# A fused attention and gated-MLP kernel: inverse root of the norm by one power operation on POOL, and other places for some steps of the third block

## Chip, core and metric

The kernel runs on one core of one Trainium2 chip. The metric is the device time of one execution in microseconds (us). TensorE is called PE here, its weight loads PEld; VectorE is DVE, ScalarE is ACT, GpSimd is POOL and SyncE is SP.

## The reference, cut to what matters

```python
def _attn_ref(q, k, v, g_norm):                  # q, k, v: (8, 8, 576, 64)
    kv = np.einsum('bhsd,bhse->bhde', k, v)
    out = np.einsum('bhsd,bhde->bhse', q, kv)
    rms = np.sqrt(np.mean(out * out, axis=-1, keepdims=True) + 1e-06)
    return out / rms * g_norm

def _moe_ref(x, w_gate, w_val, w_out, w_res):    # x: (4608, 512), d_ff 1536
    g = x @ w_gate
    gelu = 0.5 * g * (1.0 + erf(g / sqrt(2)))
    ffn_out = gelu * (x @ w_val) @ w_out
    res_gate = 1.0 / (1.0 + np.exp(-(x @ w_res)))
    return x + res_gate * ffn_out
```

Linear attention for 8 batches of 8 heads, an RMS norm over the 64 elements of each head and token, and a gated MLP with a gated residual over all 4608 tokens. The step that the change is about is the inverse root: for each token and head, (sum of squares / 64 + 1e-6) to the power of -0.5.

## The kernel before, in words

The tokens are cut into nine blocks: blocks 0 to 7 hold the first 512 tokens of each batch (NJ = 4 tiles of 128), block 8 holds the 64 tokens that each batch has left over. Every block goes through the gate and value products with a GELU, and through the output product. Matrix products from block 2 on are done with sums of quadrants (seven products in the place of eight), so DVE has to make sums of activations and weights: `ts` (token_sums, L896), `ws` (weight_sums, L870), `hid_s` (s_sum, L496).

Attention for batch b is computed two blocks ahead, in the middle of block m = b - 2 (`plan_attn_ahead`, L1389; batches 1 and 2 have plans of their own, L1314 and L1359). The order of the work is written out by hand: `at` puts a step behind a slot of a block, `aside_out` ahead of a product of the output stage (`others`, L709, with the places "F", "00", "22", "01", "11", "end"), and `at_word` behind a word of the list `ORDERS` (L911) of a group of gate and value products. There are three such groups per block. Each engine then works through its own list in that order. A step that is put earlier on DVE holds up all that stands behind it on DVE.

The words that matter: "Fg" and "Fv" are the additions of DVE in L967 that give a PSUM bank F from A and a kept tile d; "cg" and "cv" the same with the tile c; "h11", "h12", "h21" are multiplications on DVE, "h22" one on POOL (L983), which write the hidden layer; "7g" and "7v" are products of PE that write the bank that "Fg" and "Fv" have read.

The attention steps, with their lines:

- `a_sq` (L253, ACT) squares o, `a_red` (L258, DVE) sums each head into `ss`.
- `a_norm` (L295) makes `rinv` (shown as the tile `ny`) of `ss`. On POOL these are twelve instructions: L306 gives m = ss/64 + eps (tile `nm`), L307 a first guess from the bits of m, L312 to L319 two steps (tiles `na`, `nh`). On DVE there are also twelve, with three steps (L321 to L325). Batch 1 has its norm on DVE, batches 2 to 7 on POOL; for batches 3 to 7 it is put ahead of place "F" of the output stage of block b - 2.
- `a_t` (L345, DVE) multiplies a PSUM tile of o by `rinv` and writes `t`. There are four per batch, t(0) to t(3), and a fifth for the left-over rows from batch 4 on. `a_t` is the last reader of its PSUM bank: the banks of o(0) and o(1) are the banks Fg and Fv of the next block's first group.
- `d_xT` (L387) is a transposing DMA on SP's queue from `t` to `xT`; `a_g` (L370, DVE) scales `xT` in place by the norm's weight g; the products and the `ts` sums read the scaled `xT`.
- In the output stage (`others`) DVE makes wF (L714), c22 (L724, tile `osb` from `wA` and `wd`), the gatings of L698 and the `ts` sums of the next block in between; POOL makes the gating of (1,1) (L732, the tile `osb` from `th` and `osb`), which reads c22, and then `row_times_g` (L361).

The third block is block 2, the first that is done in groups throughout (`WHOLE` = 2): its attention is that of batch 2, its `ts` sums are made in the output stage of block 1, and t(2), t(3), the transposing DMA and `a_g` of batch 3 lie in its groups.

Of the kernel before, what the change touches and what calls it, by code (L numbers as in the profile page):

```python
# [7 lines left out]

FP32 = mybir.dt.float32
FP16 = mybir.dt.float16  # L10
I32 = mybir.dt.int32
AF = mybir.ActivationFunctionType
ALU = mybir.AluOpType

# [4 lines left out]
def kernel(  # L19
# [15 lines left out]
    nc = tc.nc  # L35
    P = nc.NUM_PARTITIONS
    B, H, S, D = q.shape
    C = H * D
    F = moe_w_gate.shape[1]
    NP = H // 2  # L40
    NF = F // P
    NJ = 4
# [6 lines left out]
    consts = ctx.enter_context(tc.tile_pool(name="consts", bufs=1))  # L49
# [242 lines left out]
                out=o32.rearrange("p (r e d) -> p r e d", e=2, d=D)[:, :, e, :], in_=st[b]["ps"][1][e]  # L292
            )

    def a_norm(b, j0, j1, eng=nc.vector):  # L295

        s = st[b]
        if "rinv" not in s:
            s["rinv"] = attnp.tile([P, NJ + 1, H], FP32, tag="ny", name="ny")
        ss, yy = (t[:, j0:j1, :].rearrange("p j h -> p (j h)") for t in (s["ss"], s["rinv"]))  # L300
        n = (j1 - j0) * H
        m = attnp.tile([P, (NJ + 1) * H], FP32, tag="nm", name="nm")[:, 0:n]
        a = attnp.tile([P, (NJ + 1) * H], FP32, tag="na", name="na")[:, 0:n]
        mh = attnp.tile([P, (NJ + 1) * H], FP32, tag="nh", name="nh")[:, 0:n]
        magic = 0x5F1FFFF9 if eng is nc.gpsimd else 0x5F3759DF
        eng.tensor_scalar(out=m, in0=ss, scalar1=1.0 / D, scalar2=RMS_EPS, op0=ALU.mult, op1=ALU.add)  # L306
        eng.tensor_scalar(  # L307
            out=yy.bitcast(I32), in0=m.bitcast(I32), scalar1=-0.5, scalar2=float(magic), op0=ALU.mult, op1=ALU.add
        )
        if eng is nc.gpsimd:  # L310
            for step in range(2):
                eng.tensor_tensor(out=a, in0=yy, in1=yy, op=ALU.mult)  # L312
                eng.tensor_tensor(out=a, in0=a, in1=m, op=ALU.mult)
                c = (-0.703952253, 0.703952253 * 2.38924456) if step == 0 else (0.375, -1.25)
                eng.tensor_scalar(out=mh, in0=a, scalar1=c[0], scalar2=c[1], op0=ALU.mult, op1=ALU.add)
                if step == 1:
                    eng.tensor_tensor(out=mh, in0=mh, in1=a, op=ALU.mult)
                    eng.tensor_scalar(out=mh, in0=mh, scalar1=1.875, scalar2=None, op0=ALU.add)
                eng.tensor_tensor(out=yy, in0=mh, in1=yy, op=ALU.mult)  # L319
            return  # L320
        eng.tensor_scalar(out=mh, in0=m, scalar1=-0.5, scalar2=None, op0=ALU.mult)  # L321
        for _ in range(3):
            eng.tensor_tensor(out=a, in0=yy, in1=yy, op=ALU.mult)
            eng.tensor_tensor(out=a, in0=a, in1=mh, op=ALU.mult)
            eng.scalar_tensor_tensor(out=yy, in0=a, scalar=1.5, in1=yy, op0=ALU.add, op1=ALU.mult)  # L325

    def pair(b):

# [5 lines left out]
    def a_t(b, i):  # L334

        o, rinv = st[b]["o"][i], st[b]["rinv"]
        if i < NJ:
            jj, e = i // 2, i % 2
            t = t_t[b][:, 2 * jj : 2 * jj + 2, :].rearrange("p j (r e d) -> p j r e d", e=2, d=D)[:, :, :, e, :]
            scale = of_o(rinv, i)[:, :, :, None].to_broadcast([P, 2, NP, D])  # L340
        else:
            t = t_t[B][:, pair(b), :].rearrange("p (h d) -> p h d", h=H)
            o = o.rearrange("p (h d) -> p h d", h=H)
            scale = rinv[:, NJ, :, None].to_broadcast([P, H, D])
        nc.vector.tensor_tensor(out=t, in0=o, in1=scale, op=ALU.mult)  # L345
# [17 lines left out]
    def a_g(b, j0, j1, eng=nc.vector):  # L363

        blk, k0 = where(b, j0)
        xs = xT_t[blk][:, k0 : k0 + j1 - j0, :, :]
        if eng is nc.scalar:
            nc.scalar.activation(out=xs, in_=xs, func=AF.Copy, scale=gcol)
        else:
            eng.tensor_scalar(out=xs, in0=xs, scalar1=gcol, scalar2=None, op0=ALU.mult)  # L370
# [659 lines left out]
    for which in "kv":  # L1030
        if which == "k":
            t = hidp.tile([P, NF, NJ * P], FP16, tag="hid", name=which + "f").rearrange("p a b -> p (a b)")
        else:
            t = hid_s
# [51 lines left out]
    nc.vector.memset(mask[D : 2 * D, D : 2 * D], 1.0)  # L1086
    eps_col = consts.tile([P, 1], FP32, name="eps_col")
    nc.vector.memset(eps_col, RMS_EPS)
    ones16 = consts.tile([1, P], FP16, name="ones16")
    nc.vector.memset(ones16, 1.0)  # L1090
    one32 = consts.tile([1, 1], FP32, name="one32")
# [264 lines left out]
    def aside_out(blk, ahead_of, *fs):  # L1356
        amid_out.setdefault(blk, {}).setdefault(ahead_of, []).extend(fs)

    def plan_attn_2():  # L1359
        b, m = 2, 1  # L1360
        act = nc.scalar.copy
        at(m - 1, 2 * NF + 3, lambda: by_token(b, act, slice(0, 2)))
        at(m, 0, lambda: by_token(b, act, slice(2, 4)), lambda: attn_begin(b), lambda: d_qT(b))
        at(m, 2, lambda: a_kv(b))
        at(m, 3, lambda: load_behind(b))
        at(m, 1, lambda: wo_sums(1))
        at(m, 3, lambda: wo_sums(3))
        at(m, 4, lambda: a_o(b))
        for j in range(NJ):
            at(m, 4 + j // 2, lambda j=j: a_ss(b, j))  # L1370
        at(m, 6, lambda: a_norm(b, 0, NJ, nc.gpsimd))
        for j in range(NJ):
            at(m, 9 + j // 2, lambda j=j: a_t(b, j))
        at(m, 10, lambda: d_xT(b, 0, NJ))
        for i in range(2):
            aside_out(m, "F", lambda i=i: a_g(b, 2 * i, 2 * i + 2))

    WHOLE = 2
    GROUPS = {blk: (1, 2) for blk in range(2, WHOLE)} | {blk: (0, 1, 2) for blk in range(WHOLE, B - 1)} | {B - 1: (1, 0, 2), B: (0, 1, 2)}
# [2 lines left out]
    def at_word(blk, i, word, *fs):  # L1382
        amid_gv.setdefault((blk, i), {}).setdefault(word, []).extend(fs)
# [5 lines left out]
    def plan_attn_ahead(b):  # L1389

        rem = pair(b) is not None
        m = b - 2
        assert rem == (m in GROUPS)
        act, pool = nc.scalar.copy, nc.gpsimd
        begin = [lambda: attn_begin(b), lambda: d_qT(b)]
        if rem:
            at_word(m, 0, "h22", begin.pop(0), lambda: d_rem_qT(b))
        if m in GROUPS:
            for i in range(2):
                half = lambda i=i: by_token(b, act, slice(2 * i, 2 * i + 2))  # L1400
                if whole(m):
                    at_word(m, i, "g11", half)
                else:
                    at(m, 2 + i, half)
            if whole(m):
                at_word(m, 1, "g11", *begin)
            else:
                at(m, 3, *begin)
            if b + 1 < B:
                at(m, 2 * GF, lambda: load_behind(b))  # L1410
            last = len(GROUPS[m]) - 1
        else:
            at(m, 8, lambda: by_token(b, act, slice(0, 2)))
            at(m, 9, lambda: by_token(b, act, slice(2, 4)), *begin)
            at(m, NF - 1, lambda: a_kv(b, act))
            at(m, NF, lambda: load_behind(b))
        if rem:
            at_word(m + 2, 0, "cv", lambda: a_g(b, NJ, NJ + 1))
            own = 2 * pair(b) + 1 == b
            at_word(m, last, "5v" if own else "3g", lambda: a_rem_kv(b))  # L1420
            at_word(m, last, "dv" if own else "g12", lambda: kv_out(b))
            if own:
                at_word(m, last, "3g", lambda: rem_mm(b))
            at_word(m, last, "g12", lambda: rem_out(b))
        else:
            at(m, NF, lambda: a_o(b), lambda: a_ss(b, 0), lambda: a_ss(b, 1))
            aside_out(m, "D", lambda: a_ss(b, 2), lambda: a_ss(b, 3))
        aside_out(m, "F", lambda: a_norm(b, 0, NJ + rem, pool))
        first = [lambda: new_block(b), lambda: a_t(b, 0), lambda: a_t(b, 1)]
        if whole(m + 1):  # L1430
            aside_out(m, "01" if m + 1 == WHOLE else "11", *first[0:2])
            amid_out[m].setdefault("end", []).insert(0, first[2])
        else:
            at(m, NF + 3, *first)
        if whole(m + 1):
            t = [lambda j=j: a_t(b, j) for j in range(NJ)]
            if rem:
                at_word(m + 1, 0, "h21", lambda: a_t(b, NJ), lambda: d_xT(b, NJ, NJ + 1))
            for i, word, fs in (
                (0, "1v", t[2:3]),  # L1440
                (0, "Fv", [t[3], lambda: d_xT(b, 0, NJ)]),
                (1, "cv", [lambda: a_g(b, 0, 2)]),
                (2, "Fv", [lambda: a_g(b, 2, NJ)]),
            ):
                at_word(m + 1, i, word, *fs)
            return
        for j in range(2, NJ + rem):
            at(m + 1, j - 2, lambda j=j: a_t(b, j))
        at(m + 1, 1, lambda: d_xT(b, 0, NJ))
        at_word(m + 1, 1, "Fv", lambda: a_g(b, 0, 2))  # L1450
        at_word(m + 1, 1, "cv", lambda: a_g(b, 2, NJ))
# [184 lines left out]
```

## Time and profile before

| what | us |
|---|---|
| median of 3 runs | 321.48 (321.4 to 321.97) |
| the profiled execution | 321.97, of it span 320.2 |
| PE busy | 311.9 (97% of the span) |
| DVE busy | 274.6 (86%) |
| ACT busy | 210.8 (66%) |
| POOL busy | 187.2 (58%) |
| mean granted PE clock | 0.995 |

The page gives for each engine the busy time, then the span in 40 slices, then the chain of waits that ended last, then groups of equal instructions with their mean duration and the idle time ahead of them. A timeline gives instructions in order of time: start, duration, engine, line, operation, out<-in, and in brackets the idle time before and who ended it. Ends of matmuls are modelled, so a wait of PE shows best in the distance between the starts of two groups of matmuls: four matmuls of 256 columns start 0.44 us apart from the next four when nothing holds them up, twelve start 1.31 us apart.

### The profile page before, as it was taken

Reading aid. Unit: us, or ns where it says so; the run is one execution under the profiler, and the core shown is the slowest. Engines: PE = TensorE matmul, PEld = TensorE weight load, DVE = VectorE, ACT = ScalarE, POOL = GpSimd, SP = SyncE. Lnnn points to the kernel's source line nnn. Section 1 sums busy time; section 2 is a strip of 40 time slices with the busy share of each in tenths; the row PEclk is TensorE's granted clock in tenths of the full one; section 3 lists DMA queues with packets and bytes.
Section 4 is the critical chain, followed back from the end, with each engine's and each line's share of the span. In section 5 each row is a group of like instructions: output and inputs, shape, how many; then the busy total and the mean of one; then the engine's idle time right before and its main releaser. Section 6 shows DMA issues by size and latency. Waiting matters only on the chain.

```text
span 320.2 us, 7756 instructions
## 1 busy us (share of the span) xinstructions
PE 311.9 (97%) x3044; PEld 247.5 (77%) x3044; DVE 274.6 (86%) x486; ACT 210.8 (66%) x385; POOL 187.2 (58%) x249
## 2 busy tenths in 40 slices
PE   8989999999999999999999999999999999999993
PEld 3544755444788888888888888888888888888882
DVE  5788889799888899989998999799988777897774
ACT  3673684465847795878587858795768467836760
POOL 2792350572869378757875777517761375396332
PEclk9999999999999999999999999999999999999998
DMA  8999999799994899479947894800340003001204
GB/s 251 328 204 204 195 204 190 168 155 178 176 106 82 199 130 105 82 215 120 112 82 217 109 124 69 227 6 0 69 147 2 0 3 134 0 2 44 89 2 131
DMA packets 76694, 38.90 MB, mean 122 GB/s; under 512 B 42098, under 2 KB 74354, under 8 KB 76658
## 3 DMA queue, kind: packets, MB, share of 16 engines
q0 software_dynamic: 38752, 17.17, 42.4%
q1 hardware_dynamic: 37328, 20.71, 25.3%
q8 instruction: 24, 0.39, 0.5%
q10 hardware_dynamic: 578, 0.52, 0.5%
q14 instruction: 12, 0.10, 0.1%
HBM read 38.80 MB, written 9.44 MB: 151 GB/s over the span
## 4 chain that ended last, share of the span: by engine, by line
PE 96%; DVE 2%; issue 0%; ACT 0%; DVEq 0%
PE Av L946 12%; PE Ag L946 12%; PE wA L515 12%; PE Fv L946 6%; PE Fg L946 6%; PE gps L410 5%; PE vps L410 5%; PE rA L566 4%; PE fps L447 3%; PE Ev L946 3%; PE Eg L946 3%; PE wD L515 3%; PE wF L515 3%; PE wE L515 3%; PE w L515 2%; PE idle L1111 2%
## 5 line engine op out<-in xcount | busy, mean ns | idle before, releaser
L983 POOL TENSOR_TENSOR hid<-ge,c 128x512 f16<-128x512 f16 x22 | 25.6, 1162 | 40.2 <-ACT ge L977 40.2
L515 PEld LDWEIGHTS <-hid_s 128*128 128x128 f16 x384 | 37.6, 98 | 4.5 <-issue 0.2
L946 PEld LDWEIGHTS <-wsv 128*128 128x128 f16 x352 | 34.0, 98 | 5.6 <-issue 1.3
L946 PEld LDWEIGHTS <-wsg 128*128 128x128 f16 x352 | 34.4, 98 | 4.1
L361 POOL TENSOR_TENSOR t<-t,g 128x512 f16<-128x512 f16 x32 | 37.1, 1189 | 0.0
L702 POOL TENSOR_TENSOR osb<-osb,t 128x512 f32<-128x512 f32 x28 | 34.0, 1244 | 0.0
L956 ACT COPY Eg<-Ag 128x512 f32<-128x512 f32 x22 | 12.9, 585 | 27.8 <-PE Ag L946 27.8
L515 PEld LDWEIGHTS <-hid 128*128 128x128 f16 x288 | 28.2, 98 | 3.5
L946 PEld LDWEIGHTS <-wg 128*128 128x128 f16 x264 | 25.8, 98 | 3.2
L946 PEld LDWEIGHTS <-wv 128*128 128x128 f16 x264 | 25.8, 98 | 3.0
L946 PE MATMUL Av<-ts,wsv 128*128 128x256 f16 x176 | 26.4, 272 | 0.2 <-ACT Ev L956 0.2
L946 PE MATMUL Ag<-ts,wsg 128*128 128x256 f16 x176 | 26.4, 273 | 0.0
L967 DVE TENSOR_TENSOR Fg<-Ag,d 128x512 f32<-128x512 f32 x22 | 15.3, 696 | 12.3 <-ACT d L960 7.6
L258 DVE TENSOR_REDUCE ss<-sq 128x8 f32<-128x512 f32 x32 | 20.5, 679 | 1.7 <-ACT sq L253 1.7
L398 ACT ACTIVATE ge<-gps 128x512 f16<-128x512 f32 x20 | 11.8, 599 | 14.2 <-PE gps L410 14.0
L515 PE MATMUL wA<-wo_ts,hid_s 128*128 128x256 f16 x168 | 20.6, 273 | 0.0
L977 ACT ACTIVATE ge<-Eg 128x512 f16<-128x512 f32 x22 | 13.2, 598 | 10.0 <-PE Eg L946 10.0
L977 ACT ACTIVATE ge<-c 128x512 f16<-128x512 f32 x22 | 13.8, 627 | 7.8 <-DVE c L967 7.8
L345 DVE TENSOR_TENSOR t<-op,ny 128x512 f16<-128x512 f32 x28 | 18.4, 684 | 0.5 <-POOL ny L319 0.4
L977 ACT ACTIVATE ge<-Fg 128x512 f16<-128x512 f32 x22 | 13.0, 591 | 8.6 <-PE Fg L946 6.6
L967 DVE TENSOR_TENSOR c<-Ag,d 128x512 f32<-128x512 f32 x22 | 15.2, 689 | 4.1 <-PE Ag L946 4.1
L410 PE MATMUL gps<-xT,wg 128*128 128x512 f16 x72 | 18.5, 379 | 0.0
(219 smaller groups left out, 860.2 us busy)
## 6 DMA issues: line engine op xcount, KB each, us to landing
out_dram<-osb SPq DMA_DIRECT2D x14, 512.0 KB, 3.6
qraw<-in_q_dram POOLq DMA_DIRECT2D x7, 512.0 KB, 6.8
k<-in_k_dram POOLq DMA_DIRECT2D x7, 512.0 KB, 8.7
v<-in_v_dram POOLq DMA_DIRECT2D x7, 512.0 KB, 10.5
wg<-in_moe_w_gate_dram POOLq DMA_DIRECT2D x2, 512.0 KB, 8.4
wv<-in_moe_w_val_dram POOLq DMA_DIRECT2D x2, 512.0 KB, 8.8
wo<-in_moe_w_out_dram POOLq DMA_DIRECT2D x2, 512.0 KB, 13.9
out_dram<-osb SPq DMA_DIRECT2D x4, 256.0 KB, 4.5
```

What stands on the lines that cost most here:

```text
L258: nc.vector.tensor_reduce(out=out_, in_=sqs.pop((b, i)), op=ALU.add, axis=mybir.AxisListType.X)
L345: nc.vector.tensor_tensor(out=t, in0=o, in1=scale, op=ALU.mult)
L361: eng.tensor_tensor(out=t_t[blk][:, jj, :], in0=t_t[blk][:, jj, :], in1=g16, op=ALU.mult)
L410: nc.tensor.matmul(ps[:, j0 * P : j1 * P], lhsT=w[:, cc, :], rhs=xT_t[blk][:, j0:j1, cc, :], start=(cc == 0 and j0 == 0), stop=(cc == NP - ...
L515: nc.tensor.matmul(ps[:, e - es[0], :], lhsT=a[:, f, e * P : (e + 1) * P], rhs=b[:, f, :], start=(start and e == es[0] and f == 0), stop=( ...
L566: nc.tensor.matmul(out_[:, e, :], lhsT=x_[:, e, cc, :], rhs=w_[:, cc, :], start=(first and e == 0 and cc == 0), stop=(cc == 1), skip_group ...
L702: nc.gpsimd.tensor_tensor(out=res_all[of], in0=res_all[of], in1=t_t[blk][of], op=ALU.add)
L946: nc.tensor.matmul(out_[:, r, :], lhsT=lhsT, rhs=rhs, start=(first and r == 0 and c == 0), stop=(c == 1), skip_group_check=True,)
L956: nc.scalar.copy(out=tile_of("E", u), in_=ps["A", u])
L967: nc.vector.tensor_tensor(out=dst, in0=ps["A", u], in1=sb["d", u], op=ALU.add)
L977: nc.scalar.activation(out=ge[q], in_=source(q, "g"), func=AF.Gelu)
L983: eng.tensor_tensor(out=dst, in0=ge[q], in1=source(q, "v"), op=ALU.mult)
```

## The change

- `a_norm` has two instructions in the place of twelve, both on POOL: m = ss/64 + eps, and then one tensor_tensor with the power operation, m to the power of a constant tile `minus_half`. That tile, 128x40 of -0.5, is written once by a memset on DVE in the opening.
- The norm of batch 1 moves from DVE to POOL (the default engine of `a_norm`).
- In the output stage of block 1, the two scalings `a_g` of batch 2 stood ahead of DVE's wF; they now stand behind it, ahead of the `ts` sums.
- In block 2, for batch 3: t(2) goes from behind "1v" to behind "Fv" of group 0, t(3) and the transposing DMA from behind "Fv" to behind "cv", and the first `a_g` from behind "cv" of group 1 to behind "h21" of group 1.

The instructions of PE, ACT and SP stand in the same order as before. DVE has 11 instructions fewer, POOL 58 fewer.

```diff
-    def a_norm(b, j0, j1, eng=nc.vector):
+    def a_norm(b, j0, j1, eng=nc.gpsimd):
...
         m = attnp.tile([P, (NJ + 1) * H], FP32, tag="nm", name="nm")[:, 0:n]
-        a = attnp.tile([P, (NJ + 1) * H], FP32, tag="na", name="na")[:, 0:n]
-        mh = attnp.tile([P, (NJ + 1) * H], FP32, tag="nh", name="nh")[:, 0:n]
-        magic = 0x5F1FFFF9 if eng is nc.gpsimd else 0x5F3759DF
         eng.tensor_scalar(out=m, in0=ss, scalar1=1.0 / D, scalar2=RMS_EPS, op0=ALU.mult, op1=ALU.add)
-        eng.tensor_scalar(
-            out=yy.bitcast(I32), in0=m.bitcast(I32), scalar1=-0.5, scalar2=float(magic), op0=ALU.mult, op1=ALU.add
-        )
...
-                eng.tensor_tensor(out=yy, in0=mh, in1=yy, op=ALU.mult)
-            return
...
+        eng.tensor_tensor(out=yy, in0=m, in1=minus_half[:, 0:n], op=ALU.pow)
...
+    minus_half = consts.tile([P, (NJ + 1) * H], FP32, name="minus_half")
+    nc.vector.memset(minus_half, -0.5)
...
-            aside_out(m, "F", lambda i=i: a_g(b, 2 * i, 2 * i + 2))
+            amid_out.setdefault(m, {}).setdefault("00", []).insert(i, lambda i=i: a_g(b, 2 * i, 2 * i + 2))
...
+            first_whole = m + 1 == WHOLE
             for i, word, fs in (
-                (0, "1v", t[2:3]),
-                (0, "Fv", [t[3], lambda: d_xT(b, 0, NJ)]),
-                (1, "cv", [lambda: a_g(b, 0, 2)]),
+                (0, "Fv" if first_whole else "1v", t[2:3]),
+                (0, "cv" if first_whole else "Fv", [t[3], lambda: d_xT(b, 0, NJ)]),
+                (1, "h21" if first_whole else "cv", [lambda: a_g(b, 0, 2)]),
                 (2, "Fv", [lambda: a_g(b, 2, NJ)]),
```

More of the change, by code (lines that the diff above doesn't have):

```diff
@@ L10 @@
 FP16 = mybir.dt.float16
-I32 = mybir.dt.int32
 AF = mybir.ActivationFunctionType
@@ L302, in a_norm @@
         m = attnp.tile([P, (NJ + 1) * H], FP32, tag="nm", name="nm")[:, 0:n]
-        a = attnp.tile([P, (NJ + 1) * H], FP32, tag="na", name="na")[:, 0:n]
-        mh = attnp.tile([P, (NJ + 1) * H], FP32, tag="nh", name="nh")[:, 0:n]
-        magic = 0x5F1FFFF9 if eng is nc.gpsimd else 0x5F3759DF
         eng.tensor_scalar(out=m, in0=ss, scalar1=1.0 / D, scalar2=RMS_EPS, op0=ALU.mult, op1=ALU.add)
-        eng.tensor_scalar(
-            out=yy.bitcast(I32), in0=m.bitcast(I32), scalar1=-0.5, scalar2=float(magic), op0=ALU.mult, op1=ALU.add
-        )
[L310 to L319, printed above, removed]
-            return
[L321 to L325, printed above, removed]
+        eng.tensor_tensor(out=yy, in0=m, in1=minus_half[:, 0:n], op=ALU.pow)
     def pair(b):
```

## The prediction, made before the changed kernel had run

> **What bounds the kernel now.** First the page: busy times and the 40 slices.
>
> ```profile
> PE 311.9 (97%) x3044; PEld 247.5 (77%) x3044; DVE 274.6 (86%) x486; ACT 210.8 (66%) x385; POOL 187.2 (58%) x249
> ...
> PE   8989999999999999999999999999999999999993
> ```
>
> PE is the bound from slice 3 on. A shorter norm gains nothing by itself: only a place where PE stands still can give time back. The list of waits names 0.2 us of idle PE behind the opening, but modelled ends hide more, so I read PE's timeline for starts that lie over 0.44 us (four matmuls) or 1.31 us (twelve) apart. The third block and the stage ahead of it have some:
>
> ```profile
> 86.19 1.47 PE L515 MATMUL wE<-wo,hid 128*128 128x256 f16 x12
> 87.67 1.47 PE L515 MATMUL wA<-wo_ts,hid_s 128*128 128x256 f16 x12
> ...
> 94.69 0.60 PE L946 MATMUL Ev<-xT,wv 128*128 128x256 f16 x4
> 95.25 0.60 PE L946 MATMUL Ag<-ts,wsg 128*128 128x256 f16 x4
> 95.85 0.60 PE L946 MATMUL Av<-ts,wsv 128*128 128x256 f16 x4
> ...
> 105.99 0.60 PE L946 MATMUL Ag<-ts,wsg 128*128 128x256 f16 x4
> 106.79 0.60 PE L946 MATMUL Av<-ts,wsv 128*128 128x256 f16 x4 [0.20 <-ACT Ev L956]
> ```
>
> 1.48 in place of 1.31, 0.56 and 0.60 in place of 0.44, 0.80 in place of 0.44: 0.17 + 0.12 + 0.16 + 0.36. Smaller ones at 97.63 (0.03), 105.54 (0.05) and 108.63 (0.09) make it 0.98 us. Then the output stage of a later block (2; blocks 3 to 5 look alike 32.5 us apart), DVE, POOL and PE in this order:
>
> ```profile
> 120.46 0.97 DVE L478 TENSOR_TENSOR hid_s<-hid,hid_s 128x1536 f16<-128x1536 f16 x1
> ...
> 122.64 0.68 DVE L478 TENSOR_TENSOR osb<-wA,wd 128x512 f32<-128x512 f32 x1
> ...
> 123.83 0.41 DVE L478 TENSOR_TENSOR ts<-xT,ts 128x512 f16<-128x512 f16 x1
> 124.17 0.68 DVE L698 TENSOR_TENSOR osb<-th,wF 128x512 f32<-128x512 f32 x1
> ...
> 126.00 1.28 DVE L345 TENSOR_TENSOR t<-op,ny 128x512 f16<-128x512 f32 x2
> ```
>
> ```profile
> 119.76 0.22 POOL L306 TENSOR_SCALAR nm<-ss 128x40 f32<-128x40 f32 x1 [2.15 <-DVE ss L258]
> 120.06 0.22 POOL L307 TENSOR_SCALAR ny<-nm 128x40 int32<-128x40 int32 x1
> ...
> 124.50 0.27 POOL L319 TENSOR_TENSOR ny<-nh,ny 128x40 f32<-128x40 f32 x1
> 124.73 1.27 POOL L698 TENSOR_TENSOR osb<-th,osb 128x512 f32<-128x512 f32 x1
> ```
>
> ```profile
> 126.13 0.60 PE L946 MATMUL Ag<-ts,wsg 128*128 128x256 f16 x4
> 126.74 0.60 PE L946 MATMUL Fv<-ts,wsv 128*128 128x256 f16 x4
> ```
>
> DVE works without a break from 120.46 to t(1), 126.00 to 126.69, and Fv starts 0.05 us behind it, 0.17 late (0.61 in place of 0.44): Fv's bank is that of o(1), which t(1) reads last. So in these four stages DVE's list up to t(1) is on the path that sets the end, with no slack. POOL's gating `osb<-th,osb` stands behind the norm; its input, c22, has been there since 123.32.
>
> [...]
>
> ```profile
> 281.11 0.78 DVE L478 TENSOR_TENSOR ts<-xT,ts 128x512 f16<-128x512 f16 x1
> ...
> 103.40 1.49 DVE L370 TENSOR_SCALAR xT<-xT,gcol 128x1024 f16<-128x1024 f16 x1
> ```
>
> The first takes 0.42 us by itself; a POOL multiplication ended at 281.60, and it ended 0.28 later. The second takes 0.48 elsewhere. With short POOL operations the hold is smaller (`hid_s` above met one until 120.62 and took 0.97 in place of 0.95).[...]
>
> **The change, part by part.**
>
> *The power.* Below: as cheap as a plain operation of that shape, 0.27 us (`ny<-nh,ny`, median of 12). Above: as dear as the eleven instructions that it replaces, 120.06 to 124.77, 4.7 us; nothing excludes more. A plain operation costs (1244 - 270)/(512 - 40) = 2.1 ns per element, so 40 elements are 0.08 of the 0.27 and 0.19 is fixed. I take five times the work per element: 0.19 + 0.41 = 0.6 us. The five is a choice.
>
> *Stages of blocks 2 to 5 (batches 4 to 7), in the times of block 2.* The power runs 120.06 to 120.66[...]; `hid_s`[...] starts at 120.66 in place of 120.46. Behind it, with the undisturbed steps of this list (0.90, three ts of 0.34): c22 at 122.58 to 123.26 (before 122.64: the short POOL operations had cost DVE some 0.25). Then comes the collision. `ny` is ready at 120.7, so `osb<-th,osb` no longer waits for it but starts when c22 is there (+0.09, as `nm` behind `ss`): 123.35 to 124.62. DVE's next `ts`[...] wants to start at 123.77, is held until 124.62 and ends 0.28 later, 124.90. The next starts at 124.82 (before 124.17); t(0) 125.43, gating 126.04, t(1) 126.64 to 127.33, Fv 127.38 in place of 126.74: +0.64. Four stages: **+2.6 us**. With 0.27 for the power c22 is bound by PE (122.47), Fv comes at 127.27: 4 x 0.53 = +2.1. Each further us of the power adds about 1 per stage.
>
> *Stage of block 1, third block.* wF ahead of the scalings ends by 87.2 in place of 87.61, which PE waited for (0.17). The scalings then wait for the power (86.61 to 87.21) and end near 88.1, two ts near 88.8, c22 starts at 88.9 when PE lets it, 0.4 ahead of need. POOL's gating runs near 89.7 to 91[...]. t(2) behind "Fv": "Fg" starts 0.6 earlier, which 7g and 7v waited for (0.12, 0.16, 0.03). t(3) 1.2 later, and its DMA with it: landings take at most 6.3, and `a_g` comes 8 us later; on SP's queue nothing due stands behind it. `a_g` out of "cv": the hidden products no longer stand behind 1.49 us, Ev's seed is in time (0.05, 0.36, 0.09). At "h21" it meets POOL's `hid` (105.14 to 106.3 before) and ends just as "Fg" may start; I take **-0.9** of the 0.98.
>
> *Batch 1.* The chain on DVE runs 47.54 to 49.97, t at 50.07. On POOL: `nm` at 47.61, power 47.91 to 48.51, t near 48.6. PE's transposes stand behind a run of output matmuls and start at 51.46 without a gap: nothing gained. Nothing lost up to a power of 2.1 us; from there each us is lost on PE. POOL is idle there from 44.8 to 55.3, only the store's additions stand behind. DVE waits in t, ahead of the sums of w_out, which now come earlier.
>
> *Batch 2.* t starts at 74.70, 0.7 behind `ny`: no gain, no loss.
>
> *The memset*: at most 0.11 us (a 64x64 one); hidden by the warm-up matmuls ahead of PE's first transposes at 5.84; without that cover 0.1.
>
> Sum: +2.6 - 0.9 = +1.7. The profiled execution (span 320.2, time 321.97, 0.49 above the median) would become 323.7; on the median 321.48 + 1.7 = **323.2**. A measurement here can tell about 0.2%, 0.64 us.
>
> **The rivals.**
>
> *A. Faster: the gating doesn't hold `ts`* (it starts too late[...]). For it: DVE is up to 0.3 us ahead by then, and short POOL operations hold it little. Against: four `ts` near 280 were each held by POOL multiplications. Then t(1) ends some 0.1 earlier than before: -0.9 - 4 x 0.1 = -1.3, **320.2**. It decides at Fv: below +0.22 us per stage (0.9/4) the kernel gets faster.
>
> *B. No change*: held in part, +0.2 per stage: -0.1, 321.4.
>
> *C. The power is slow.* For it: no operation of this kind is in the trace[...]; against: nothing. At 2.0 us `hid_s` starts at 122.06, t(1) ends at 128.73, Fv +2.04, four times 8.2; c22 of block 1 is late by 0.75: +8.05, **329.5**. At 4.7 us it is some 4.7 per stage, 3 in block 1 and 2.6 for batch 1: near 345.
>
> **How the numbers follow.** Forecast (power 0.27 to 1.2 us, collision) 0.48, from 322.7 to 325.6; A 0.14; B 0.11; C 0.27. Range 320.8 to 330: it leaves out half of A and half of C. Faster 0.14, same 0.11, slower 0.75.
>
> **What would show it.** POOL's `osb<-th,osb` near 123.4 and the `ts` behind it 1.1 us long; Fv of the first group over 1 us behind Ag; `hid_s` at the power's end; PE's late starts of the third block gone. A power over 1.2 us, or a `ts` of 0.42 us there, would make the forecast wrong.

## The result, and the profile after

The changed kernel takes 334.35 us (median of 4 runs, 333.31 to 338.45) against 321.46. It is 1.0387 times as long, 95% interval 1.034 to 1.0433; this ratio leaves out the slow run of 338.45, whose granted clock was 0.983 in place of 0.996. The forecast was 323.2 with 320.8 to 330 as its range, slower with 0.75. The direction was right and the time was missed by 11 us. The profiled execution took 333.31 us, 11.34 us more than that of before, with a span of 331.5.

PE's work is the same (311.7 us busy, before 311.9), and its share has dropped:

```profile
PE 311.7 (94%) x3044; PEld 246.8 (74%) x3044; DVE 272.4 (82%) x475; ACT 210.4 (63%) x385; POOL 208.5 (63%) x191
...
PE   8899996999989997999799998999799999999993
```

In the row of slices 6, 7 and 8 stand where 9 stood, six times: PE stands still at six places inside the span. POOL is busier by 21 us, although it has 58 instructions fewer. The view of the tile `ny` says why; its columns are least, median and largest duration in ns:

```profile
L303 POOL TENSOR_TENSOR ny<-nm,minus_half x7: 5457/6764/6788, 47.2 to 227.2; 128x40 f32<-128x40 f32 x4, 128x32 f32<-128x32 f32 x3
```

One power takes 5.46 us for 32 columns and 6.78 us for 40: longer than the eleven instructions that it replaced (4.7 us). What that does is seen in the output stage of block 2, the one shown for before (3.05 us later here: `nm` at 122.81 against 119.76). First POOL, then DVE, then PE:

```profile
122.81 0.22 POOL L302 TENSOR_SCALAR nm<-ss 128x40 f32<-128x40 f32 x1 [2.11 <-DVE ss L257]
123.11 6.79 POOL L303 TENSOR_TENSOR ny<-nm,minus_half 128x40 f32<-128x40 f32 x1
129.88 1.26 POOL L676 TENSOR_TENSOR osb<-th,osb 128x512 f32<-128x512 f32 x1
```

```profile
123.51 0.95 DVE L456 TENSOR_TENSOR hid_s<-hid,hid_s 128x1536 f16<-128x1536 f16 x1
...
126.70 0.42 DVE L456 TENSOR_TENSOR ts<-xT,ts 128x512 f16<-128x512 f16 x1
127.04 0.68 DVE L676 TENSOR_TENSOR osb<-th,wF 128x512 f32<-128x512 f32 x1
129.93 0.69 DVE L323 TENSOR_TENSOR t<-op,ny 128x512 f16<-128x512 f32 x1 [2.22 <-POOL ny L303]
```

```profile
128.31 0.60 PE L924 MATMUL Av<-xT,wv 128*128 128x256 f16 x4
130.68 0.60 PE L924 MATMUL Fg<-ts,wsg 128*128 128x256 f16 x4 [1.77 <-DVE t L323]
131.11 0.60 PE L924 MATMUL Ag<-ts,wsg 128*128 128x256 f16 x4
131.88 0.60 PE L924 MATMUL Fv<-ts,wsv 128*128 128x256 f16 x4 [0.16 <-DVE t L323]
```

t(0) waits 2.22 us for the power. Before, it started without a wait:

```profile
124.80 0.69 DVE L345 TENSOR_TENSOR t<-op,ny 128x512 f16<-128x512 f32 x1
```

The bank of t(0) is the bank of Fg, so Fg starts 2.37 us behind Av in place of 0.44, and Fv waits another 0.33 for t(1). DVE's list ahead of that wait runs undisturbed: `hid_s` starts 0.40 us into the power and takes 0.95, `ts` takes 0.42. Where batch 1's norm now stands on POOL, PE's transposes wait as well (timeline of PE, 46 to 56 us; first before, then after):

```profile
51.46 0.61 PE L352 MATMUL xtp<-ident,t 128*128 128x128 f16 x8
```

```profile
54.08 0.62 PE L330 MATMUL xtp<-ident,t 128*128 128x128 f16 x8 [3.12 <-DVE t L323]
```

The sum over the span, from the distances between the starts of PE's matmuls in the two profiles:

| where | before | after | difference, us |
|---|---|---|---|
| batch 1, transposes | 0 | 3.29 | +3.29 |
| first group of block 2: Fg, Ag, Fv | 0.04 | 1.47 | +1.43 |
| first groups of blocks 3 to 6: Fg, Fv | 0.70 | 9.03 | +8.33 |
| late starts ahead of and in the third block | 0.98 | 0 | -0.98 |
| opening, up to 20 us | 7.33 | 6.63 | -0.71 |

Together +11.36 of the 11.34. The opening's share is not of the change: it varies between runs of one kernel (7.33 us in the profile of before, 7.44 in that of e11, 6.64 in that of e7, which share its opening). The large terms are all waits of t for the power.

### The profile page after: what moved, and what is told of

The parts are those of the page before. It is cut to its first block, busy times and chain, and to the rows that moved or that the text cites. A ratio compares the mean times of both kernels' runs of the same rounds, so it can differ in the third digit from the quotient of the medians.

```text
span 331.5 us, 7687 instructions
## 1 busy us (share of the span) xinstructions
PE 311.7 (94%) x3044; PEld 246.8 (74%) x3044; DVE 272.4 (82%) x475; ACT 210.4 (63%) x385; POOL 208.5 (63%) x191
## 4 chain that ended last, share of the span: by engine, by line
PE 73%; DVE 9%; POOL 8%; ACT 3%; issue 2%; DMA 2%; SPq 1%; DVEq 0%; POOLq 0%; ACTq 0%
PE Ag L924 11%; PE Av L924 11%; POOL ny L303 8%; PE Fv L924 6%; PE Fg L924 6%; PE wA L493 5%; PE gps L388 5%; PE vps L388 5%; PE rA L544 3%; PE Ev L924 3%; PE Eg L924 3%; PE w L493 2%; PE rps L408 2%; PE rF L544 2%; PE kvp L207 2%
## 5 line engine op out<-in xcount | busy, mean ns | idle before, releaser
L303 POOL TENSOR_TENSOR ny<-nm,minus_half 128x40 f32<-128x40 f32 (+1 forms) x7 | 43.5, 6216 | 0.6
L924 PE MATMUL Fg<-ts,wsg 128*128 128x256 f16 x88 | 13.2, 272 | 7.4 <-DVE t L323 7.4
```

The lines of the kernel that those rows point to most:

```text
L303: eng.tensor_tensor(out=yy, in0=m, in1=minus_half[:, 0:n], op=ALU.pow)
L924: nc.tensor.matmul(out_[:, r, :], lhsT=lhsT, rhs=rhs, start=(first and r == 0 and c == 0), stop=(c == 1), skip_group_check=True,)
```

## The experiments

Theory 1: the loss is the time at which `ny` is ready for t, and nothing else; the other places of the third block's steps gain about 0.9 us. The first rival was the forecast's own mechanism, the collision of POOL's early gating with DVE's `ts`; the second, that the power's long run holds DVE or POOL's later work. All ratios are to the kernel before on the same chip.

**e1_places: the places without the power.** The kernel before with the two parts of the diff that move steps:

```diff
-            aside_out(m, "F", lambda i=i: a_g(b, 2 * i, 2 * i + 2))
+            amid_out.setdefault(m, {}).setdefault("00", []).insert(i, lambda i=i: a_g(b, 2 * i, 2 * i + 2))
...
-                (0, "1v", t[2:3]),
+                (0, "Fv" if first_whole else "1v", t[2:3]),
...
```

> The third block's other places alone; the norm stays as before (guess and steps, batch 1 on DVE). Theory 1 (all of the loss is the wait for the power): the late starts of PE ahead of and in the third block (0.98 us in the profile of before) go, about 0.9 us faster than before, 320.5. Rival (the places themselves cost something, or gain nothing): 321.5 or more.

Measured 0.997 (0.9956 to 0.9984), 320.99 against 321.8: as theory 1 expected. The same kernel ran once more for a profile.

**e11_places_again: the same kernel.**

> The third block's places alone once more, for a profile of it beside that of before: the late starts of PE at wA behind wE, at 7g and 7v of group 0 and at Av behind Ev's seed (0.98 us in the profile of before) are gone, and 0.997 of before as in the first series; if the gain comes from elsewhere, these starts are still late.

Measured 0.9965 (0.9948 to 0.9983). The same places in PE's timeline as in the prediction (0.9 to 1.0 us later here at the first of them), where the starts were 1.48, 0.56, 0.60 and 0.80 us apart:

```profile
87.15 1.47 PE L515 MATMUL wE<-wo,hid 128*128 128x256 f16 x12
88.46 1.47 PE L515 MATMUL wA<-wo_ts,hid_s 128*128 128x256 f16 x12
...
95.47 0.60 PE L946 MATMUL Ev<-xT,wv 128*128 128x256 f16 x4
95.91 0.60 PE L946 MATMUL Ag<-ts,wsg 128*128 128x256 f16 x4
96.35 0.60 PE L946 MATMUL Av<-ts,wsv 128*128 128x256 f16 x4
...
106.39 0.60 PE L946 MATMUL Ag<-ts,wsg 128*128 128x256 f16 x4
106.83 0.60 PE L946 MATMUL Av<-ts,wsv 128*128 128x256 f16 x4
```

1.31, 0.44, 0.44 and 0.44: all four are gone. This version, guess and steps with the new places, is faster than both kernels; it takes 0.35% less time than the one before.

**e2_power: the power without the places.** The changed kernel with those two parts of the diff taken back.

> The power operation alone, all places as before. Theory 1: the loss of the changed kernel and the gain of the places that is then missing, +12.5 to +13 us on before, about 334.2. Rival (part of the loss comes from the places): less than +12, below 333.5.

Measured 1.0504 (1.0481 to 1.0526), 338.11 us: more than either theory expected. The row of PE's clock in its page, and PE's timeline at the two places where a digit of it drops:

```profile
PEclk9999997999999999999999997999999999999998
```

```profile
54.80 1.03 PE L330 MATMUL xtp<-ident,t 128*128 128x128 f16 x8 [3.13 <-DVE t L323]
55.63 1.91 PE L425 MATMUL fps<-wo,hid 128*128 128x512 f16 x4
```

```profile
204.20 1.01 PE L924 MATMUL Fv<-ts,wsv 128*128 128x256 f16 x4 [0.16 <-DVE t L323]
205.00 1.06 PE L924 MATMUL Av<-ts,wsv 128*128 128x256 f16 x4
205.86 1.06 PE L924 MATMUL Eg<-xT,wg 128*128 128x256 f16 x4
```

Four matmuls of 256 columns take 0.86 us in place of 0.44 here. PE's granted clock was 0.51 from 54.00 to 57.50 us (PE still waited, until 54.80) and 0.50 from 204.20 to 207.60, and 1.00 from 57.50 to 61.00 and from 201.00 to 204.20. By the distances between the starts of matmuls the two stretches cost 1.28 and 1.67 us. The profiled execution of the changed kernel has no such stretch (1.00 from 20 to 320 us), and this one's span is 4.9 us longer. The rest of the 4.9 is the missing gain of the places (1.0 us in its profile: 0.16 + 0.13 + 0.16 + 0.37 and three starts below 0.1), 0.1 at Fg of the first group of block 2, and 0.75 in the opening. So the places' gain holds with the power too; the clock was in neither theory.

**e3_product: a short operation in the power's place.** The inverse root is left out.

```diff
-        eng.tensor_tensor(out=yy, in0=m, in1=minus_half[:, 0:n], op=ALU.pow)
+        eng.tensor_tensor(out=yy, in0=m, in1=minus_half[:, 0:n], op=ALU.mult)
```

> The changed kernel with a product in the place of the power: same instructions, queues and waits, but ny is -m/2, so the inverse root is left out and the output is not the reference's. It is the short operation of 0.27 us that my forecast reckoned with. Theory 1 (only the time at which ny is ready counts): no loss is left and the places' gain stays, 320.6 or less. Rival (the collision of the forecast: the gating on POOL starts earlier and holds the ts sum of DVE in four stages, 0.53 us each): 322.7, with ts rows of about 1.1 us near the gating.

Measured 1.003 (1.0017 to 1.0043), 322.91 us against 321.8. A product of the same tiles takes 0.27 us (median of seven) where the power took 6.78, and most of the loss is gone. But the rival came true: with a `ny` that is ready early the kernel is still slower than before, although it keeps the places' gain. DVE and POOL in the output stage of block 2, then PE:

```profile
121.44 0.68 DVE L676 TENSOR_TENSOR osb<-th,wE 128x512 f32<-128x512 f32 x1
122.03 1.17 DVE L456 TENSOR_TENSOR ts<-xT,ts 128x512 f16<-128x512 f16 x1
123.13 0.67 DVE L676 TENSOR_TENSOR osb<-th,wF 128x512 f32<-128x512 f32 x1
```

```profile
121.66 1.27 POOL L676 TENSOR_TENSOR osb<-th,osb 128x512 f32<-128x512 f32 x1 [2.94 <-issue]
```

```profile
123.64 0.60 PE L924 MATMUL Av<-xT,wv 128*128 128x256 f16 x4
124.46 0.60 PE L924 MATMUL Fg<-ts,wsg 128*128 128x256 f16 x4 [0.22 <-DVE t L323]
124.89 0.60 PE L924 MATMUL Ag<-ts,wsg 128*128 128x256 f16 x4
125.65 0.60 PE L924 MATMUL Fv<-ts,wsv 128*128 128x256 f16 x4 [0.16 <-DVE t L323]
```

POOL's gating no longer stands behind a long norm and starts at 121.66. DVE's `ts`, 0.42 us by itself, takes 1.17: it ends 0.27 behind the gating's end (122.93). Fg comes 0.38 late and Fv 0.33, together 0.71 in place of 0.17: +0.53 per stage. The forecast's step for the cheapest power had +0.53.

**e8_product_sum_end: the same with the collision taken away.** The fourth `ts` sum goes from place "01" to "end", behind t(1); the inverse root is left out as in e3.

```diff
-        for key, f in zip(("00", "00", "22", "01") if whole(blk) else ("00", "22", "01", "11"), t):
+        for key, f in zip(("00", "00", "22", "end") if whole(blk) else ("00", "22", "01", "11"), t):
```

> The product in the place of the power (the inverse root left out, as before), and the fourth ts sum moved behind t(1), out of the way of the early gating. Collision theory: the 0.38 + 0.33 us at Fg and Fv of four stages (2.8 us) go, 322.5 - 2.8 = 319.7; up to 320.7 if the sum is now held by the multiplications by g behind the gating and makes Fg late. Rival (these late starts are not of the held sum): 322.5.

Measured 0.9971 (0.9959 to 0.9984): the late starts at Fg and Fv are gone in all four stages, a smaller one (0.16 at a later Av) has come. In the stage of block 2:

```profile
124.17 0.60 PE L924 MATMUL Av<-xT,wv 128*128 128x256 f16 x4
124.61 0.60 PE L924 MATMUL Fg<-ts,wsg 128*128 128x256 f16 x4
125.04 0.60 PE L924 MATMUL Ag<-ts,wsg 128*128 128x256 f16 x4
125.48 0.60 PE L924 MATMUL Fv<-ts,wsv 128*128 128x256 f16 x4
```

The loss of e3 was the collision's.

**e4_split: the power in two instructions.**

```diff
-        eng.tensor_tensor(out=yy, in0=m, in1=minus_half[:, 0:n], op=ALU.pow)
+        for c in (slice(0, 2 * H), slice(2 * H, n)):
+            eng.tensor_tensor(out=yy[:, c], in0=m[:, c], in1=minus_half[:, c], op=ALU.pow)
```

> The changed kernel with the power in two instructions, first the 16 columns that t(0) and t(1) read, then the rest: as much work on POOL and one instruction more. By the two shapes measured, 5.46 us for 32 and 6.78 for 40 columns, 16 take about 2.8 us. Theory 1 (the time at which t(0) and t(1) get their ny): in the four stages ny is there 2.8 us behind nm, ahead of need, so their 2.27 us each go; batch 1 keeps 2 to 3 us; in all 322 to 323.5. Rival (the time that POOL is busy or holds DVE counts): no faster than the changed kernel, about 333.

Measured 1.0158 (1.0135 to 1.0182), 327.26 us. POOL is as busy as in the changed kernel (210.8 us), and 7 us have gone: not POOL's load but the time of `ny` counts. It is 4 us above my expectation, which had left out the second half of the columns. DVE in the stage of block 2, where the second power ends at 128.67:

```profile
127.31 0.68 DVE L324 TENSOR_TENSOR t<-op,ny 128x512 f16<-128x512 f32 x1
128.70 0.69 DVE L324 TENSOR_TENSOR t<-op,ny 128x512 f16<-128x512 f32 x1 [0.71 <-POOL ny L304]
```

t(2) now waits, with the additions Fg and Fv behind it on DVE, and PE's next products start 0.21 and 0.17 late. Three more starts are late in block 3 (0.09 to 0.31) and in each of blocks 4 to 6 (0.13 to 0.26); their cause is not followed here. Batch 1 keeps 0.77 + 1.56 us at its two transposes.

**e6_first_on_dve: batch 1's norm back on DVE.**

```diff
-            NF + 6: [lambda: a_norm(b, 0, NJ), t[0], t[1], t[2], t[3]],
+            NF + 6: [lambda: a_norm(b, 0, NJ, nc.vector), t[0], t[1], t[2], t[3]],
```

with the guess and the three steps for DVE in `a_norm` again.

> The changed kernel with the norm of batch 1 on DVE by guess and steps again, as before; the power for batches 2 to 7. Theory 1 (each norm's loss is its own wait): the 3.3 us that PE stands still ahead of batch 1's transposes go, 333.3 - 3.3 = 330.0. Rival (batch 1's loss is caught up later, or the power's load counts elsewhere): 332 or more.

Measured 1.0325 (1.0287 to 1.0362), 332.3 us, 330.44 to 334.21. In its profile the late start of the transposes is gone, all 3.29 us of it, and the terms of the other batches are the same to about 0.01 us; but it has one stretch of half clock (1.67 us; the granted clock of its span is 0.991 in place of 0.996) and a start 0.7 late near 43 us that the profile of the changed kernel lacks, so its span is only 0.9 shorter. The lowest runs of the two kernels differ by 2.9 us, about the 3.3 expected; the medians by 2.05. By times alone the size is only roughly confirmed, and the rival's 332 isn't excluded by them; the profile decides for theory 1.

**e7_sum_end and e9_sum_fv: can the faster version gain more?** e11 with the fourth `ts` sum at "end" (as in e8), or behind "Fv" of the next block's first group.

The edit of e9:

```diff
-        for key, f in zip(("00", "00", "22", "01") if whole(blk) else ("00", "22", "01", "11"), t):
+        for key, f in zip(("00", "00", "22", "Fv") if whole(blk) else ("00", "22", "01", "11"), t):
+            if key == "Fv":
+                at_word(blk, 0, key, f)
+                continue
```

> Guess and steps, the new places, and the fourth ts sum moved behind t(1). DVE's list up to t(1) is 0.34 us shorter in four stages, and Fv starts 0.17 late there: 4 x 0.17 = 0.7 faster than the places alone (0.997 of before), 0.995. Rival (the sum meets POOL's multiplications by g at its new place, is held up to 1.2 us and makes Fg late): 0.997 or more.

> As the one before, but the fourth ts sum stands behind Fv of the next block's first group, ahead of t(3), where DVE's list has some slack. Expected 0.995 of before; if the sum is held there by POOL's multiplications and makes the c tiles late, 0.997 or more.

Measured 0.9993 (0.9971 to 1.0015) and 1.0049 (1.0033 to 1.0065): the rival in both. In e7 the late start of Fv (0.17) is gone, but the sum meets POOL's multiplications by g; DVE and then POOL:

```profile
124.77 0.78 DVE L478 TENSOR_TENSOR ts<-xT,ts 128x512 f16<-128x512 f16 x1
```

```profile
124.11 4.69 POOL L361 TENSOR_TENSOR t<-t,g 128x512 f16<-128x512 f16 x4
```

The sum takes 0.78 us in place of 0.42, the addition Fg comes later, and two later products of PE start 0.15 and 0.17 late: 0.32 for 0.17. Behind "Fv" it is worse, 0.62 + 0.17 per stage. By these profiles the place before the change is the best of the three for this sum, when the norm is slow enough to keep the gating out of its way.

**e10_power_one: another exponent.** The inverse root is left out again, as the exponent is 1.

```diff
-    nc.vector.memset(minus_half, -0.5)
+    nc.vector.memset(minus_half, 1.0)
```

> The changed kernel with an exponent of 1.0 in the place of -0.5 (so ny is m and the inverse root is left out). If the power's price is that of the operation and the number of columns, its rows stay at 5.5 us for 32 and 6.8 for 40 columns; if it depends on the exponent, they are shorter, and the kernel with them.

Measured in a single run: 5.46 us for 32 columns, 6.78 for 40, time 333.53 us. With the pieces of e4 (2.93 us for 16 columns, at most 4.17 for 24) the price is some 0.16 us per column, and for 32 and 40 columns the same with both exponents.

## Why the prediction was wrong, by its own steps

- *"I take five times the work per element: 0.19 + 0.41 = 0.6 us. The five is a choice."* This is the step that failed. Measured 6.78 us for 40 columns: 0.16 us per column, some 80 times the 2.1 ns that the forecast had worked out from the plain operations of before. Even the upper value of the step, 4.7 us, which was only the price of what was replaced, was too low. Nothing in the profile of before bore on it, so a slow power deserved more than the 0.27 of rival C. Both signs that the forecast had named against itself came: a power over 1.2 us, and a `ts` of 0.42.
- *"The power runs 120.06 to 120.66 ... `hid_s` ... starts at 120.66."* This step failed too. The profile of before shows DVE held by POOL's multiplications and additions (0.78 us in place of 0.42, 1.49 in place of 0.48); that a power holds it as well was the author's estimate. `hid_s` and four `ts` ran beside the power at 0.95, 0.42, 0.43, 0.42 and 0.42 us. The power costs by the wait of t(0) alone: from 120.06, in the times of before, 6.78 us put `ny` at 126.84, 2.04 behind the start of t(0) (124.80), and the stages lost 2.1 each. Rival C had let the power hold `hid_s` for as long as it runs, some 4.7 us on each stage at 4.7 us of power, so its time for a slow power (345) came out too high, while the range, which ended near a power of 2 us, was too low. By the forecast's own "about 1 per stage" for each further us, the measured price would have given about 4 x (0.64 + 6.2) = 27 us in place of the 8.33 measured.
- *The collision of the gating with `ts`.* Right where it applies, and it doesn't apply in the changed kernel: `ny` was ready so late that the gating came 3 us behind the `ts`. So "slower" came true without the mechanism that the forecast gave for it; that part was luck. With a short operation (e3) it stands as worked out: 1.17 us for the `ts` (forecast about 1.1), +0.53 per stage, total 1.003.
- *Third block, "-0.9 of the 0.98".* Right: 0.997 and 0.9965 by themselves, all late starts gone.
- *Batch 1: "Nothing lost up to a power of 2.1 us; from there each us is lost on PE."* Right: 5.47 - 2.1 = 3.4, measured 3.29.
- *Batch 2 and the memset.* DVE waited 0.17 us for batch 2's late `ny` (77.54) and started its t 0.03 behind it; no late start of PE there. The memset took 0.09 us on DVE and cost nothing that shows.

So theory 1 accounts for the loss of the profiled execution, and the forecast's sum lacked nothing else larger than 0.1 us there. In e2 and e6 stretches at half clock came on top (1.28 and 1.67 us, 1.67 us), which neither had. A run of the changed kernel with a granted clock of 0.991 in place of 0.996 was 2.0 us longer than the profiled one. That it had one such stretch, of some 1.7 us, is an estimate from those of e2 and e6.

## What to carry to other kernels

An operation that no row of the profile shows has no known price, and fewer instructions are no argument: run it first by itself, at the shape wanted; one row of one run would have told 6.8 us here. When an engine off the path gets faster, look for what it releases: with the short product of e3, the gating on POOL that had waited for the norm ran into DVE's sum (1.17 us in place of 0.42), and cost twice what the places had gained. A step belongs in the list behind those whose results PE waits for; the few steps that were moved back in the third block gave 0.3% by themselves.

## What was not expected of the hardware

- The power on POOL: 2.93, at most 4.17, 5.46 and 6.78 us for 16, 24, 32 and 40 columns of 128 partitions in fp32; for 32 and 40 columns the same with the exponents -0.5 and 1.0.
- It did not hold the operations of DVE that ran beside it. `hid_s` took 0.95 us within a power of 6.79, and 0.947 to 0.957 in all its 32 rows of the changed kernel; two scalings `a_g` took 0.87 together, as before, within a power of 5.46. Three of POOL's operations of 512 columns did hold one of DVE: beside the gating a `ts` took 1.17 us in place of 0.42 (e3), beside the multiplications by g 0.78 (e7), and beside the additions of before a scaling took 1.49 in place of 0.48 (shown in the prediction). What sets the power apart from them is not shown. The power and the two scalings of the changed kernel:

```profile
89.24 5.46 POOL L303 TENSOR_TENSOR ny<-nm,minus_half 128x32 f32<-128x32 f32 x1
```

```profile
89.70 0.87 DVE L348 TENSOR_SCALAR xT<-xT,gcol 128x1024 f16<-128x1024 f16 x2
```

- Half a clock behind waits of PE, in the profile of e2 and not in that of the changed kernel. Ahead of its two stretches PE had waited: 3.13 us for t in front of the transposes at 54.80, with the clock at half from about 54.0 on, and 1.93 + 0.33 = 2.26 us at Fg and Fv of the stage at 203.00, with the clock at half from about 204.2 on. The profile of the changed kernel has the same waits, 3.12 us at 54.08 and 1.93 + 0.33 in the stages at 130.68, 165.29 and 199.90, and a granted clock of 1.00 from 20 to 320 us. So waits of the same sizes came with half a clock in one execution and without it in another; what decides is not shown. The stretches cost 1.28 and 1.67 us in e2 and 1.67 in e6 on top of the waits, and times scatter: 333.31, 333.37 and 335.33 us in three executions of the changed kernel.
